# Third batch's keys taken into the second chunk's steps, and every second weight tile of layer 2 finished on GpSimd

## The chip, the cores and the metric

The kernel runs on one core of a Trainium2 chip. The core has TensorE (PE, matmuls and transposes into PSUM banks), VectorE (DVE), ScalarE (ACT), GpSimd (POOL) and SyncE (SP), which issues every DMA of this kernel from one queue. Each engine works through its own queue in order and waits on semaphores. The metric is the device time of one execution in microseconds.

## The reference

Eight batches of attention, whose keys and values are first averaged over groups of eight rows (576 rows become 72), feed two layers of the same shape: 4608 tokens, 512 wide, through 2048 and back.

```python
k_p = k.reshape(B, H, Sp, pool, D).mean(axis=3)      # v_p likewise
scores = scale * np.matmul(q, k_p.transpose(0, 1, 3, 2))
attn = softmax(scores);  x = np.matmul(attn, v_p)    # B*S = 4608 tokens, H*D = 512
h = np.maximum(x @ w_in, 0.0);   x = h * h @ w_out   # layer 1
h = x @ w_in2                                        # layer 2
g = np.where(h >= 1, h, np.where(h <= -1, 0.0, (h + 1) ** 2 / 4))
out = g @ w_out2
```

q, k and v are float32. The four weight matrices come as float64, so the kernel decodes them from their 64-bit words; each float32 factor of a large product is split into a rounded half and its residue, and three matmuls stand for one.

## The kernel before

**Tiling.** The 4608 tokens are nine chunks of 512 (`NC`). A batch has 576 tokens, so its border falls inside a chunk: the second chunk (tokens 512 to 1023) and the third (1024 to 1535) each span two batches. For each chunk and layer the 2048 inner columns are 16 steps (`KF`) of 128. A step is `h_mm` (L627: 12 matmuls, hp) and, two steps behind (`LAG`), `y1_mm` or `y2_mm` (L666, L677: 12 matmuls into the four result banks y0 to y3). Two hp banks alternate. Between the products stand the activation and the split: `act1` (L638: three ScalarE passes and one VectorE instruction, L652) in layer 1, `act2` (L655: three ScalarE passes, two VectorE instructions, L661 and L663) in layer 2. A result bank leaves through `y_out` (L686), alternately by ScalarE and VectorE, into one of two `yo` buffers and by a store; layer 1's result goes to DRAM (`x2T`) and comes back for layer 2 by `load_x2` and `split_x2` (L717).

**Weights.** Class `Weights` handles one layer. Tile f holds the 128 columns of w_in and the 128 rows of w_out of step f. `load` (L227) brings 1 MB by two DMAs into the slot of tile f; layer 2's tile f lies in layer 1's slot f - 1, so its load waits for the last product that reads layer 1's tile f - 1 (tile 0 has a buffer of its own, xb). `decode0` is two ScalarE passes (L256, L263), `decode1` four VectorE instructions (L269, L272, L275, L278), `split_hi` one ScalarE pass (L285), and `split_lo` (L288) one VectorE instruction, L290, the last of a tile: 1024 columns, both inputs and the output in SBUF. `stages` (L293) runs them as a pipeline: one `step` does split_hi of tile k - 1, decode0 of tile k + 1, decode1 of tile k, and split_lo of tile k - 1 inside that decode1. The first step does decode0 of tiles 0 and 1.

**Stages.** The opening (to about 177 us) does the first chunk's attention, layer 1's weights, the first chunk of layer 1, and the second chunk's attention, in an order that a list planner (`Order`, L49) chose from assumed durations and from the events that each chain waits for. Keys of a batch are loaded (`load_k`, L332, 288 KB for two heads) into one buffer `kv`, averaged by three GpSimd additions (`k_pool`, L365 to L369), then transposed and scaled (`k_T`, L379). `v_pool` and `v_split` do the like for values. In the planner's chain `keys1` (L869) the second batch's keys and values are followed by the third batch's four key pairs and its first value load. From the second chunk of layer 1 on, the attention of the next chunk is placed by hand: `attention_units` (L722) gives each unit a position in steps, and the main loop (L1034) emits those that are due (`do`) twice a step. In the last chunk of layer 1 the loop also calls `w2.load_to(f)` and, from step index 3 (`STEPS2`) on, `w2.step()`; in layer 2's first chunk the remaining steps follow, one per step (L1075).

Of the kernel before, what the change touches and what calls it, by code (L numbers as in the profile page):

```python
# [14 lines left out]
ALU = mybir.AluOpType  # L15
# [33 lines left out]
class Order:  # L49
# [13 lines left out]
    def add(self, gen, rank=0.0):  # L63
        c = [rank, self.now, gen, None, None]
        self.chains.append(c)
        self.go(c)
# [57 lines left out]
def pooled_attention_moe_moe2(  # L124
# [13 lines left out]
    nc = tc.nc  # L138
# [5 lines left out]
    NP = H // 2  # L144
# [30 lines left out]
    for d in range(2):  # L175
        m = mask[64 * d:64 * d + 64]
        nc.gpsimd.affine_select(
            out=m, in_=m, compare_op=ALU.is_ge, fill=0.0, base=0, channel_multiplier=1, pattern=[[-KL, H]]
        )
        nc.gpsimd.affine_select(  # L180
            out=m, in_=m, compare_op=ALU.is_ge, fill=0.0, base=KL - 1, channel_multiplier=-1, pattern=[[KL, H]]
# [7 lines left out]
    for c in range(NC):  # L189
        gs, col = [], 0  # L190
        while col < N:
            t0_ = c * N + col
            b, s = t0_ // S, t0_ % S
            n = min(S - s, N - col, NG)
# [12 lines left out]
    def w_tile(f, dtype, name):  # L207
        return wpool.tile([P, 4 * DM], dtype, tag=f"w{f}", name=name)

    class Weights:  # L210
# [76 lines left out]

        def split_lo(self, f, t):  # L288
            av = self.a.pop(f).rearrange("p (w n) -> p w n", w=2)
            nc.vector.tensor_tensor(out=t[:, :, 1], in0=av, in1=t[:, :, 0], op=ALU.subtract)  # L290
            self.ready.add(f)

        def stages(self):  # L293
# [35 lines left out]
    def kv_tile():  # L329
        return att.tile([P, 2, POOL * D], F32, tag="kv", name="kv")  # L330

    def load_k(b, p, t=None):  # L332

        t = kv_tile() if t is None else t
        nc.sync.dma_start(
            out=t[:SP_], in_=k[b, 2 * p:2 * p + 2].rearrange("h (s r) d -> s h (r d)", r=POOL)
        )
        kraw[b, p] = t

    def load_v(b, g, t=None):  # L340

        t = kv_tile() if t is None else t
        for e in range(2):
            r = slice(64 * e, 64 * e + 64)
            if g < 2:
                src = v[b, 4 * g + e:4 * g + e + 3:2, :KA * POOL, :]
                nc.sync.dma_start(out=t[r], in_=src.rearrange("h (s r) d -> s h (r d)", r=POOL))
            else:
                src = v[b, :, KA * POOL:, :]
                nc.sync.dma_start(out=t[r, 0], in_=src.rearrange("h (s r) d -> h s (r d)", r=POOL))  # L350
        vraw[b, g] = t
# [9 lines left out]
    def pool8(eng, t, dst):  # L361
        us = (("POOL", 1.3), ("POOL", 0.8), ("POOL", 0.7)) if eng is nc.gpsimd else (
            ("DVE", 0.7), ("DVE", 0.45), ("DVE", 0.3))
        yield us[0]
        eng.tensor_tensor(out=t[:, :, :256], in0=t[:, :, :256], in1=t[:, :, 256:], op=ALU.add)  # L365
        yield us[1]
        eng.tensor_tensor(out=t[:, :, :128], in0=t[:, :, :128], in1=t[:, :, 128:256], op=ALU.add)
        yield us[2]
        eng.tensor_tensor(out=dst, in0=t[:, :, :64], in1=t[:, :, 64:128], op=ALU.add)  # L369
# [3 lines left out]
    def k_pool(b, p, eng):  # L373
        kp = att.tile([P, 2, D], F32, tag="kp", name="kp", bufs=4)
        t, dst = kraw.pop((b, p))[:SP_], kp[:SP_]
        yield from pool8(eng, t, dst)
        kp_t[b, p] = kp
# [14 lines left out]
    def v_pool(b, g, eng):  # L392
        t = vraw.pop((b, g))
        w = 2 if g < 2 else 1
        vp = att.tile([P, 2, D], F32, tag="vp", name="vp") if b else lent[7][:, 0, 2 * D * g:2 * D * g + 2 * D]
        if b == 0:
            vp = vp.rearrange("p (a d) -> p a d", d=D)
        vp_t[b, g] = vp
        yield from pool8(eng, t[:, :w], vp[:, :w])
# [45 lines left out]
    w1, w2 = Weights(0), Weights(1)  # L445
# [3 lines left out]
    def at_once(chain):  # L449

        if chain is None:
            return
        value = None
        while True:
            try:
                kind, x = chain.send(value)
            except StopIteration:
                return
            value = None
            if kind == "take":  # L460
                value = order.things[x].pop(0)[1]
# [260 lines left out]
    def attention_units(c, at, stage=(0, 0.5, 1, 1, 2, 2.5, 3)):  # L722

        units = []
        ts = tiles[c]

        def add(s, f, *a):
            units.append((s, lambda: at_once(f(*a))))

        for i, T in enumerate(ts):  # L730
            s = at[i]
            if i:
                add(at[i - 1] + 0.5, load_q, T)
            else:
                add(s - 2, load_q, T)
            add(s + stage[0], t0, T)
            add(s + stage[1], t1, T, 0)
            add(s + stage[1], t1, T, 1)
            add(s + stage[2], t3, T)
            add(s + stage[3], t4, T)  # L740
            add(s + stage[4], t56, T)
            G = T.group
            if T is G.tiles[-1]:
                for p in range(NP):
                    add(s + stage[5 + p // 2], pv_pair, G, p)
            if i + 1 < len(ts) and ts[i + 1].b != T.b:

                b = T.b + 1
                a = s + stage[1]
                if b > 2:  # L750
                    add(a - 7, load_k, b, 0)
                for p in range(NP):
                    if b > 2:
                        add(a - 6 + 1.5 * p, k_pool, b, p, nc.gpsimd)
                        if p + 1 < NP:
                            add(a - 6 + 1.5 * p, load_k, b, p + 1)
                        else:
                            add(a - 6 + 1.5 * p, load_v, b, 0)
                    add(a + 0.5 + p // 2 * 0.5, k_T, b, p)
                e = s + stage[6]  # L760
                add(a, v_pool, b, 0, nc.gpsimd)
                add(a, load_v, b, 1)
                add(e, v_split, b, 0, nc.gpsimd)
                add(e, v_pool, b, 1, nc.gpsimd)
                add(e, load_v, b, 2)
                add(e + 1, v_split, b, 1, nc.gpsimd)
                add(e + 1, v_pool, b, 2, nc.gpsimd)
                add(e + 1.5, v_split, b, 2, nc.gpsimd)
        return units

    STEPS2 = 3

    SCALAR = range(2, 9)

    with tc.manual_schedule():

        lent = []
        for i in range(4):
            t = w_tile(KF - 4 + i, F32, "lent").rearrange("p (e a n) -> p e a n", e=2, a=2)
# [7 lines left out]
        t = w_tile(8, F32R, "lent")  # L787
# [7 lines left out]
        def comes(us):  # L795

            landed[0] = max(landed[0], order.now) + us
            return landed[0] + 2.0
# [70 lines left out]
        def keys1():  # L869
            for p in range(NP):  # L870
                load_k(1, p)
                yield "until", comes(1.3)
                yield from k_pool(1, p, nc.gpsimd)
                order.signal("kp", p)
            for g in range(3):
                load_v(1, g)
                yield "until", comes(2.2)
                yield from v_pool(1, g, nc.gpsimd)
                yield ev("x", G1[0])
                yield from v_split(1, g, nc.gpsimd)  # L880
            for p in range(NP):
                load_k(2, p)
                yield "until", comes(1.3)
                yield from k_pool(2, p, nc.gpsimd)
            load_v(2, 0)

        def keys1_T():
            yield ev("scores", T1[0])
# [134 lines left out]
        units = []  # L1023
        for c in range(2, NC):
            n = len(tiles[c])
            stride = 3 if n > 4 else 3.5
            units += attention_units(c, [16 * (c - 1) - 1 + stride * i for i in range(n)])
        units.sort(key=lambda u: u[0])

        def do(s):  # L1030
# [3 lines left out]
        for c in range(1, NC):  # L1034
            last = c + 1 == NC
            for f in range(KF):
                hp = h_mm(x_of(c), W[0, 0, f])
                outs(2)
                do(KF * c + f)
                if last and f == 0:  # L1040
                    att_cm.__exit__(None, None, None)
                    l2 = ctx.enter_context(tc.tile_pool(name="l2", bufs=1))
                if f >= LAG:
                    y_step(0, c, f - LAG)
                elif f == 0:
                    y_step(0, c - 1, KF - 1)
                at_once(act1(hp, c, f))
                outs(2)
                if last:
                    w2.load_to(f)  # L1050
                    if f == 3:
                        xraw = load_x2(0)
                    if f >= STEPS2:
                        w2.step()
                    if f in (8, 10, 12, 14):
                        split_x2(0, xraw, (8, 10, 12, 14).index(f))
                do(KF * c + f + 0.5)
            y_step(0, c, KF - 2)
            if last:
                w2.load_to(KF)  # L1060
# [58 lines left out]
```

## Time and profile before

| | |
|---|---|
| median of 3 runs | 1794.53 us (1792.99 to 1795.15) |
| the profiled execution's own time | 1792.96 us |
| its span | 1791.2 us |
| PE busy | 1743.7 us, 97% |
| DVE busy | 739.7 us, 41% |
| ACT busy | 781.4 us, 44% |
| POOL busy | 158.2 us, 9% |
| mean granted TensorE clock | 0.987 |

A row of the profile's views gives a start and a duration in us, counted from the span's start; "L290" is a line of the kernel, out<-in are tiles by name. A bracket behind a row is the time for which the engine stood idle before it, and what ended that. DVE's busy time is not even: in the 40 slices of the span (44.8 us each) it stands at 70%, 90% and 90% in the first three, at 20% to 40% in most, and at 90% and 80% in the two from 940 to 1030 us. Matmuls overlap, so a matmul's own duration (0.39) is longer than its place in the queue (0.23).

### The profile page before, as it was taken

What the parts mean: (1) busy time and instruction counts of PE and PEld (TensorE: products, weight loads), DVE (VectorE), ACT (ScalarE), POOL (GpSimd) and SP (SyncE); (2) the same over time, 40 slices, a digit from 0 to 9 for tenths busy, and PEclk for the clock granted to TensorE, in tenths of its full rate; (3) what the DMA queues carried; (4) which work ended last, traced back from release to release, by engine and by line L of the source; (5) the groups of instructions that cost most, each with busy time, mean ns of one, the idle gap of its engine ahead of it and who ended that gap; (6) DMA issues with size and microseconds to landing.
All of it is one profiled execution on the core that took longest, in us unless ns stands there. A gap on an engine that the chain in (4) does not pass through costs nothing.

```text
span 1791.2 us, 20650 instructions
## 1 busy us (share of the span) xinstructions
PE 1743.7 (97%) x8116; PEld 1442.2 (81%) x8116; DVE 739.7 (41%) x1234; ACT 781.4 (44%) x1499; POOL 158.2 (9%) x183
## 2 busy tenths in 40 slices
PE   5898999999999999999999999999999999999999
PEld 4676788888888888888888788888888888888887
DVE  7995433434243333433339832232332323233222
ACT  5874434434343343344348633333333333334333
POOL 3333211202021110300000000000000000000000
PEclk6999999999999999999999999999999999999999
DMA  9643201102021121201045301010101010101000
GB/s 252 182 123 100 55 23 53 41 26 65 13 70 28 50 48 34 52 18 36 1 142 196 133 1 47 1 47 1 47 1 47 1 47 1 48 1 48 0 24 24
DMA packets 89601, 95.18 MB, mean 53 GB/s; under 512 B 43296, under 2 KB 61984, under 8 KB 89504
## 3 DMA queue, kind: packets, MB, share of 16 engines
q1 hardware_dynamic: 89504, 93.87, 17.9%
q8 instruction: 64, 1.05, 0.2%
q14 instruction: 33, 0.27, 0.1%
HBM read 73.66 MB, written 20.19 MB: 52 GB/s over the span
## 4 chain that ended last, share of the span: by engine, by line
PE 87%; DVE 8%; DMA 2%; issue 2%; ACT 1%; SPq 0%; DVEq 0%; ACTq 0%
PE hp L633 14%; PE hp L634 13%; PE hp L635 13%; PE y L684 7%; PE y L682 7%; PE y L683 7%; PE y L671 7%; PE y L672 6%; PE y L675 6%; PE pvps L611 2%; PE sps L502 2%; DVE w L290 1%; DVE wa L275 1%; DVE wa L278 1%; DVE wa L269 1%
## 5 line engine op out<-in xcount | busy, mean ns | idle before, releaser
L633 PE MATMUL hp<-x,w 128*128 128x512 f32 x1116 | 442.5, 396 | 4.9 <-ACT w L285 2.7
L634 PE MATMUL hp<-x,w 128*128 128x512 f32 x1116 | 436.4, 391 | 0.6 <-DVE w L290 0.5
L635 PE MATMUL hp<-x,w 128*128 128x512 f32 x1116 | 436.6, 391 | 0.0
L633 PEld LDWEIGHTS hp<-x,w 128*128 128x128 f32 x1116 | 210.6, 189 | 49.5 <-ACT w L285 3.1
L661 DVE SCALAR_TENSOR_TENSOR u<-u,hp 128x512 f32<-128x512 f32 x144 | 99.0, 687 | 359.7 <-ACT u L660 359.7
L635 PEld LDWEIGHTS hp<-x,w 128*128 128x128 f32 x1116 | 210.4, 189 | 44.7
L634 PEld LDWEIGHTS hp<-x,w 128*128 128x128 f32 x1116 | 210.6, 189 | 42.8 <-DVE w L290 1.4
L671 PE MATMUL y<-gh,w 128*128 128x512 f32 x576 | 231.3, 402 | 0.0
L652 DVE TENSOR_TENSOR gl<-hp,gh 128x512 fp32r<-128x512 f32 x144 | 99.4, 690 | 310.7 <-ACT hp L650 310.5
L672 PE MATMUL y<-gh,w 128*128 128x512 f32 x576 | 225.1, 391 | 0.0
L659 ACT ACTIVATE u<-hp 128x512 f32<-128x512 f32 x144 | 85.9, 596 | 286.8 <-PE hp L635 286.8
L684 PE MATMUL y<-w,gl 128*128 128x512 f32 x540 | 210.2, 389 | 0.0
L682 PE MATMUL y<-w,gh 128*128 128x512 f32 x540 | 210.2, 389 | 0.0
L683 PE MATMUL y<-w,gh 128*128 128x512 f32 x540 | 210.1, 389 | 0.0
L662 ACT ACTIVATE gh<-u 128x512 fp32r<-128x512 f32 x144 | 91.0, 632 | 173.5 <-PE y L683 148.9
L663 DVE TENSOR_TENSOR gl<-u,gh 128x512 fp32r<-128x512 f32 x144 | 99.8, 693 | 157.8 <-ACT gh L662 152.2
L675 PE MATMUL y<-gl,w 128*128 128x512 f32 x576 | 154.4, 390 | 0.0
L648 ACT ACTIVATE gh<-hp 128x512 fp32r<-128x512 f32 x144 | 86.2, 598 | 120.3 <-PE y L672 119.4
L641 ACT ACTIVATE hp<-hp 128x512 f32<-128x512 f32 x144 | 85.0, 591 | 99.5 <-PE hp L635 99.2
L675 PEld LDWEIGHTS y<-gl,w 128*128 128x128 f32 x576 | 108.1, 188 | 23.0
L671 PEld LDWEIGHTS y<-gh,w 128*128 128x128 f32 x576 | 108.3, 188 | 21.0
L672 PEld LDWEIGHTS y<-gh,w 128*128 128x128 f32 x576 | 108.4, 188 | 20.3
(140 smaller groups left out, 2004.9 us busy)
## 6 DMA issues: line engine op xcount, KB each, us to landing
w<-in_moe_w_in_dram SPq DMA_DIRECT2D x31, 512.0 KB
w<-in_moe_w_out_dram SPq DMA_DIRECT2D x31, 512.0 KB
x2T<-yo SPq DMA_DIRECT2D x36, 256.0 KB
xraw<-x2T SPq DMA_DIRECT2D x9, 1024.0 KB
out_dram<-yo SPq DMA_DIRECT2D x35, 256.0 KB
qraw<-in_q_dram SPq DMA_DIRECT2D x32, 256.0 KB
kv<-in_k_dram SPq DMA_DIRECT2D x28, 288.0 KB
kv<-in_v_dram SPq DMA_DIRECT2D x28, 256.0 KB
```

The costliest lines, as they stand in the source:

```text
L633: nc.tensor.matmul(out=hp, lhsT=hi[:, cs], rhs=xh[kk], start=(kk == 0), stop=False)
L634: nc.tensor.matmul(out=hp, lhsT=lo[:, cs], rhs=xh[kk], start=False, stop=False)
L635: nc.tensor.matmul(out=hp, lhsT=hi[:, cs], rhs=xl[kk], start=False, stop=(kk == KD - 1))
L652: nc.vector.tensor_tensor(out=gl, in0=hp, in1=gh, op=ALU.subtract)
L661: nc.vector.scalar_tensor_tensor(out=u, in0=u, scalar=1.0, in1=hp, op0=ALU.min, op1=ALU.max)
L663: nc.vector.tensor_tensor(out=gl, in0=u, in1=gh, op=ALU.subtract)
L671: nc.tensor.matmul(out=ys[d], lhsT=hi[:, cs], rhs=gh, start=(f == 0), stop=False)
L672: nc.tensor.matmul(out=ys[d], lhsT=lo[:, cs], rhs=gh, start=False, stop=False)
L675: nc.tensor.matmul(out=ys[d], lhsT=hi[:, cs], rhs=gl, start=False, stop=(f == KF - 1))
L682: nc.tensor.matmul(out=ys[t], lhsT=gh[:, cs], rhs=hi, start=(f == 0), stop=False)
L683: nc.tensor.matmul(out=ys[t], lhsT=gh[:, cs], rhs=lo, start=False, stop=False)
L684: nc.tensor.matmul(out=ys[t], lhsT=gl[:, cs], rhs=hi, start=False, stop=(f == KF - 1))
```

## The change

`split_lo` of layer 2 goes to GpSimd for odd tiles. `STEPS2` falls from 3 to 2, so that the first `w2.step()` comes in the third step of layer 1's last chunk instead of the fourth, and tile 0 is loaded in the first step of it instead of the second. The third batch's key loads, key averages and first value load leave `keys1`; `attention_units` emits them for batch 2 too, starting with the second chunk's first step, 1.25 steps apart, and the third chunk's tokens from the second on are put about three steps later.

```diff
@@ -287,7 +287,9 @@
 
         def split_lo(self, f, t):
             av = self.a.pop(f).rearrange("p (w n) -> p w n", w=2)
-            nc.vector.tensor_tensor(out=t[:, :, 1], in0=av, in1=t[:, :, 0], op=ALU.subtract)
+
+            eng = nc.gpsimd if self.layer and f % 2 else nc.vector
+            eng.tensor_tensor(out=t[:, :, 1], in0=av, in1=t[:, :, 0], op=ALU.subtract)
             self.ready.add(f)
 
         def stages(self):
@@ -747,17 +749,22 @@
 
                 b = T.b + 1
                 a = s + stage[1]
-                if b > 2:
-                    add(a - 7, load_k, b, 0)
+                e = s + stage[6]
+                if b == 2:
+
+                    k0, gap, kt = s, 1.25, [s + 2.5 + 1.25 * p for p in range(NP)]
+                    a, e = s + 6, s + 7
+                else:
+                    k0, gap, kt = a - 7, 1.5, [a + 0.5 + p // 2 * 0.5 for p in range(NP)]
+                add(k0, load_k, b, 0)
                 for p in range(NP):
-                    if b > 2:
-                        add(a - 6 + 1.5 * p, k_pool, b, p, nc.gpsimd)
-                        if p + 1 < NP:
-                            add(a - 6 + 1.5 * p, load_k, b, p + 1)
-                        else:
-                            add(a - 6 + 1.5 * p, load_v, b, 0)
-                    add(a + 0.5 + p // 2 * 0.5, k_T, b, p)
-                e = s + stage[6]
+                    sp = (k0 + 0.5 if b == 2 else k0 + 1) + gap * p
+                    add(sp, k_pool, b, p, nc.gpsimd)
+                    if p + 1 < NP:
+                        add(sp, load_k, b, p + 1)
+                    else:
+                        add(sp, load_v, b, 0)
+                    add(kt[p], k_T, b, p)
                 add(a, v_pool, b, 0, nc.gpsimd)
                 add(a, load_v, b, 1)
                 add(e, v_split, b, 0, nc.gpsimd)
@@ -768,7 +775,7 @@
                 add(e + 1.5, v_split, b, 2, nc.gpsimd)
         return units
 
-    STEPS2 = 3
+    STEPS2 = 2
 
     SCALAR = range(2, 9)
 
@@ -878,11 +885,6 @@
                 yield from v_pool(1, g, nc.gpsimd)
                 yield ev("x", G1[0])
                 yield from v_split(1, g, nc.gpsimd)
-            for p in range(NP):
-                load_k(2, p)
-                yield "until", comes(1.3)
-                yield from k_pool(2, p, nc.gpsimd)
-            load_v(2, 0)
 
         def keys1_T():
             yield ev("scores", T1[0])
@@ -1024,7 +1026,10 @@
         for c in range(2, NC):
             n = len(tiles[c])
             stride = 3 if n > 4 else 3.5
-            units += attention_units(c, [16 * (c - 1) - 1 + stride * i for i in range(n)])
+            at = [16 * (c - 1) - 1 + stride * i for i in range(n)]
+            if c == 2:
+                at[1:] = [at[0] + 6.5 + 3 * i for i in range(n - 1)]
+            units += attention_units(c, at)
         units.sort(key=lambda u: u[0])
 
         def do(s):
@@ -1047,7 +1052,7 @@
                 at_once(act1(hp, c, f))
                 outs(2)
                 if last:
-                    w2.load_to(f)
+                    w2.load_to(f or 1)
                     if f == 3:
                         xraw = load_x2(0)
                     if f >= STEPS2:
```

## Rows read from the trace of the kernel before

**Rows 1.** Busy time by stretch: length, then PE, PEld, DVE, ACT, POOL busy, clock, DMA.

```profile
922.40:1003.99 81.59, 81.59 (x362) 67.56 (x360) 73.64 (x85) 67.33 (x89) 0.00 (x0) 1.00 0.61 209
1003.99:1030.10 26.11, 22.69 (x98) 17.79 (x97) 22.21 (x28) 16.38 (x23) 0.00 (x0) 1.00 0.24 81
```

**Rows 2.** Timeline of DVE in layer 1's last chunk: start, duration, instruction.

```profile
934.05 0.69 DVE L652 TENSOR_TENSOR gl<-hp,gh 128x512 fp32r<-128x512 f32 x1 [0.66 <-ACT hp L650]
...
940.12 0.69 DVE L269 TENSOR_SCALAR wa<-wa 128x1024 f32<-128x1024 f32 x1
...
941.45 1.22 DVE L290 TENSOR_TENSOR w<-wa,w 128x1024 fp32r<-128x1024 f32 x1
942.58 1.22 DVE L275 SCALAR_TENSOR_TENSOR wa<-w,wa 128x1024 int32<-128x1024 int32 x1
943.83 1.23 DVE L278 CUSTOM_DVE_ANT_0 wa<-w,wa 128x2048 uint16<-128x2048 uint16 x1
...
945.58 0.68 DVE L269 TENSOR_SCALAR wa<-wa 128x1024 f32<-128x1024 f32 x1
```

**Rows 3.** Groups by line, 929.3 to 1003.9: busy us, mean ns of one.

```profile
L256 ACT ACTIVATE wa<-w 128x1024 f32<-128x1024 f32 x13 | 14.9, 1143 | 0.0
...
L641 ACT ACTIVATE hp<-hp 128x512 f32<-128x512 f32 x12 | 7.0, 585 | 0.0
L720 DVE TENSOR_TENSOR x<-xraw,x 128x512 fp32r<-128x512 f32 x4 | 2.7, 685 | 0.0
```

**Rows 4.** Timeline of PE: a first product that needs the bank back.

```profile
938.71 0.39 PE L633 MATMUL hp<-x,w 128*128 128x512 f32 x1
```

**Rows 5.** Timeline of DVE in layer 2's first steps.

```profile
1004.56 0.68 DVE L269 TENSOR_SCALAR wa<-wa 128x1024 f32<-128x1024 f32 x1
...
1012.00 0.69 DVE L269 TENSOR_SCALAR wa<-wa 128x1024 f32<-128x1024 f32 x1
...
1018.92 0.69 DVE L269 TENSOR_SCALAR wa<-wa 128x1024 f32<-128x1024 f32 x1
```

**Rows 6.** Timeline of DVE in the opening, beside POOL.

```profile
32.57 2.24 DVE L278 CUSTOM_DVE_ANT_0 wa<-w,wa 128x2048 uint16<-128x2048 uint16 x1
...
144.63 1.75 DVE L275 SCALAR_TENSOR_TENSOR wa<-w,wa 128x1024 int32<-128x1024 int32 x1
```

**Rows 7.** Timeline of POOL: two rows beside DVE, two with DVE idle.

```profile
32.46 1.26 POOL L365 TENSOR_TENSOR kv<-kv 72x512 f32<-72x512 f32 x1 [6.42 <-DMA kv<-in_k_dram]
...
143.70 1.60 POOL L367 TENSOR_TENSOR kv<-kv 72x256 f32<-72x256 f32 x1
...
175.44 1.29 POOL L365 TENSOR_TENSOR kv<-kv 128x512 f32<-128x512 f32 x1 [20.32 <-DMA kv<-in_v_dram]
176.81 0.74 POOL L367 TENSOR_TENSOR kv<-kv 128x256 f32<-128x256 f32 x1
```

**Rows 8.** Timeline of SP's queue: tile 1 of layer 2.

```profile
922.58 0.38 SPq L232 DMA_DIRECT2D w<-in_moe_w_in_dram  x1
```

**Rows 9.** Busy time by stretch: last two numbers DMA share and GB/s.

```profile
927.00:928.00 1.00, 1.00 (x6) 0.84 (x5) 0.00 (x0) 0.82 (x2) 0.00 (x0) 1.00 0.17 70
```

**Rows 10.** Chain that ended last: start, length, piece.

```profile
124.92 5.32 DMA x1S<-xs
...
188.20 2.03 DMA x2T<-yo
```

**Rows 11.** Timeline of SP's queue in the opening.

```profile
124.14 0.50 SPq L335 DMA_DIRECT2D kv<-in_k_dram  x1
```

**Rows 12.** Timeline of ACT in the opening, with its wait.

```profile
130.35 0.39 ACT L619 ACTIVATE xs<-pvps 128x256 fp32r<-128x256 f32 x1 [3.26 <-DMA x1S<-xs]
```

**Rows 13.** Timeline of PE: waits in the opening and the second chunk's start.

```profile
139.94 0.63 PE L560 MATMUL aps<-ident,A 128*128 128x128 f32 x4 [1.87 <-DVE A L541]
...
182.86 0.26 PE L383 MATMUL kps<-ident,kp 72*128 72x72 f32 x1 [0.64 <-DVE E L521]
183.72 0.25 PE L383 MATMUL kps<-ident,kp 72*128 72x72 f32 x1 [0.60 <-DVE E L521]
```

## The prediction, made before the change was run

> **What bounds the kernel now.** I read four views, in this order: busy time by stretch, VectorE's instructions in order of time, GpSimd's beside them, and the chain of waits at the two places where TensorE stands still. TensorE works through 288 steps, each a first-product group and a second-product group of 12 matmuls. From 922.40 to 1003.99, in the last chunk of layer 1, 30 groups take 81.59 us: 2.72 each, 5.44 a step, with no gap [rows 1]. The next eight groups, over the seam into layer 2, take 26.11 where 8 x 2.72 = 21.76 would do, so 4.3 us are lost there [rows 1]; behind the seam the steps are whole again. The other loss lies in the opening. The two halves of the change touch one of them each.
>
> In the last chunk VectorE, not TensorE, is full. One step of it runs from the clamp at 940.12 to the next at 945.58, which is 5.46 us without a hole, and the instruction that the change moves (L290) holds the queue for 942.58 - 941.45 = 1.13 [rows 2]. Four of the steps carry one more instruction (L720), 0.60 each at its spacing [rows 3]. VectorE therefore loses 0.02 a step and 4 x 0.60 = 2.4 on TensorE. That is paid from slack: the residue (L652) that ends at 934.05 + 0.69 = 934.74 is first missed by the matmul at 938.71, 3.97 later [rows 2, 4]. In layer 2 the same decode meets a longer activation: VectorE's steps there go from 1004.56 to 1012.00 to 1018.92, 7.44 and 6.92 [rows 5], and this overrun is the 4.3 lost.
>
> **Layer 2's weights: GpSimd's instruction.** Eight of 16 tiles lose 1.13 us of VectorE's queue each, 9.0 in all. GpSimd's 128x512 addition takes 1.29 and its 128x256 one 0.74 when VectorE is idle [rows 7]; 0.55 per 256 columns more makes 1.29 + 2 x 0.55 = 2.39 for 1024 columns, which I take. What it does to VectorE is seen in the opening. While GpSimd's addition held 32.46 to 33.72, VectorE's L278, issued at 32.57, took 2.24 where it takes 1.23 alone; it ended at 34.81, about one clean duration after GpSimd's end [rows 6, 7]. L275 at 144.63 took 1.75 where its clean row has 1.22 [rows 2, 6]; GpSimd's L367 beside it, which had waited for VectorE in its turn, took 1.60 instead of 0.74 [rows 7]. So the two exclude one another, whole instructions at a time, for each of the decode's VectorE instructions that the rows show beside GpSimd. With VectorE always ready, an odd tile costs it 2.39 and saves 1.13: +1.26. The lower bound lets GpSimd run under the one residue per step that reads PSUM (0.60), a block of 1.79 and +0.66; below nothing it goes only if VectorE has holes, which is a rival.
>
> The GPSIMD Engine Reference of the Trainium skill (section "Performance versus the Vector engine") gives 4497 ns for such an addition over 2048 columns; half of it, 2.25, is an estimate from that page, and would make the layer-2 term below about 7.8 instead of 8.7.
>
> **Layer 2's weights: one step earlier.** Decoding from the third step gives VectorE one more step, but not a free one. Tile 1's slot is released when a second product ends, so its load leaves at 922.58 in either kernel [rows 8]; the transfer is at work until 927.2 or so [rows 9]. Today ScalarE comes to that tile a step later and finds it there. After the change ScalarE's in-order queue stands at it with the next step's three activation passes behind it, then that step's residue on VectorE. Two decode passes of 1.14 and three of about 0.59 [rows 3] put the third step's residue near 927.2 + 2.3 + 1.8 = 931.3. The fourth's stands behind that one (0.60) and a decode of 4.86 (5.46 less 0.60), near 936.7, which is 2.7 later than the row at 934.05 [rows 2]. Slack falls from 3.97 to 1.3. If the 1 MB input load that is issued just behind tile 2 delays it too, to about 0.1. Every later load is also waited for, with less than a step to spare. Tile 0's load, moved forward a step, goes between the stores of the chunk before, two issues of the size of the 0.38 in [rows 8], and I cost it at nothing. Nothing else is on GpSimd's queue by then. TensorE now waits on GpSimd for odd tiles, but first reads each one several steps after it is made, and ScalarE, which takes a tile's buffer over for the third tile after it, comes three steps later.
>
> **Sum for the seam.** Eleven steps remain in layer 1, 5.5 pairs. A pair has 2 x 5.46 + 1.26 = 12.18 on VectorE against 10.88 on TensorE: 5.5 x 1.30 = 7.2, and 2.4 for L720, less 1.3 of slack, is 8.3 of waiting already in layer 1, where today there is none. In layer 2 two decodes are left instead of three: (7.44 + 1.26 - 5.44) + (6.92 - 5.44) = 4.7. Together 13.0, less today's 4.3: **+8.7**. With a block of 1.79 the same sum gives 5.5 x 0.70 + 2.4 - 1.3 + 4.1 = 9.1, or **+4.8**. With late loads and the clean duration simply doubled (2.58), 8.2 + 2.4 - 0.1 + 4.9 = 15.4, or **+11**.
>
> **The keys: what leaves the opening.** Four key loads, a value load and twelve GpSimd additions leave. Two things there stand on the path to the last weight tile. A store of layer-1 input, issued at 124.92 right behind a key load of 124.14, needed 5.32 to land, where a store of the same size took 2.03 [rows 10, 11]; ScalarE stood 3.26 for it [rows 12], and TensorE later 1.87 for what follows [rows 13]. I take 1.87 of that as won, TensorE being otherwise busy. And VectorE's 0.53 at 144.63 goes [rows 6]. Together -2.4; at the least -0.5 (the store is slow by itself), at the most -3.8 (3.26 and 0.53). In the first step of the second chunk two key transposes sit on TensorE's queue and wait 0.64 and 0.60 for score banks [rows 13]. They now come steps later, one by one: -1.24, or 0 if another wait takes their place there.
>
> **The keys: what is added.** The same loads and additions in steps 16 to 22. GpSimd is idle there, and its additions at 1.29 + 0.74 and less collide with little on VectorE; I cost them at nothing. SyncE's queue is the cover to watch: each next key load waits for the addition that frees the one buffer, and the stores of layer 1's output are behind it, and behind these the four result banks of the next chunk. A landing of some 3 us and additions of 2.5 fit in the 5.44 between two such loads; at the bound, the landing of 5.32 [rows 10] with 2.5, each is 2.4 late, of which one would reach the banks: +2.4.
>
> **Total.** -2.4 - 1.24 + 8.7 = +5.1 on the profiled execution's own 1792.96 us (a span of 1791.2 and 1.8 around it), which is 1798.0. The median of the runs is 1794.53, 1.57 above that execution, so the forecast is 1799.6.
>
> **Rivals.** *GpSimd's instruction hides.* If VectorE has holes of its own while it waits for loads and for ScalarE, the block fills them and the whole 1.13 is won. The Perfetto Trace Analysis page of the Trainium skill ("Optimizing Scalar/DVE Operations") says that when VectorE is saturated, offloading, even to GpSimd, may help, and adds that between these two it might not; the rows here bear out the second. Against it: 5.46 of 5.44 us in use, and whole-instruction blocks. For it: eleven more steps with load waits. A microsecond less of block is worth 6.5 in the sum (5.5 pairs and the first step of layer 2), so the layer-2 part is zero at a block of 2.39 - 8.7/6.5 = 1.05, and the total at 2.39 - 5.1/6.5 = 1.6; below that the change is faster. Unblocked, most of the 4.3 goes: (7.44 - 1.13 - 5.44) is left in the first step, about -3.4, and with the keys' -3.6 the time is 1787.5. *The keys give nothing and the block binds.* The opening's store is as slow without the key load, or the moved loads hold SyncE's queue: 1794.53 + 8.7 - 0.5 = 1802.7, and with the moved loads' 2.4, 1805.1. *A near draw.* Block at its lower bound (+4.8), and the opening at its best (-3.8 - 1.24): 1794.5.
>
> **How the numbers follow.** The forecast's mechanism, with blocks of 1.79 to 2.58, has 0.58; its own range is 1794.5 (the draw's ends) to 1804 (+11 with -0.5 - 1.24). The hidden instruction has 0.20, keys that give nothing 0.12, the draw 0.10. About 0.2% (3.6 us) is what a measurement of this kernel can tell from no change. Slower by more: 0.40 of the 0.58 and the 0.12, so 0.52. Faster by more: 0.18 of the 0.20 and 0.06 of the draw, where more of the opening's waits close than I count: 0.24. Within: 0.24. The range reaches down to the hidden case and up past late keys: 1787.5 to 1806.
>
> **What would show it.** In the changed profile: VectorE's decode instructions of 3 us and more (1.2 plus a block) beside each GpSimd L290-like subtraction of about 2.4 in the last chunk; gaps on TensorE before first products from about two thirds of that chunk on; more than 4.3 lost at the seam; ScalarE waiting for a weight load in every step from the third on; in the opening no wait for a store near 127 to 130, and the last tile's load issued 2 to 3 us earlier. It would be wrong if VectorE's instructions keep their 1.2 beside GpSimd's, or if the steps of the last chunk stay at 5.44 to their end.

## The result, and the profile after

The changed kernel takes 1808.39 us (median of five runs, 1801.70 to 1809.11) beside 1795.15 for the kernel before (1792.99 to 1798.56): a ratio of 1.0058, interval 1.0044 to 1.0073, so 10.4 us slower. Run a second time beside other runs of before it gave 1.0052 (1.0035 to 1.0068), 9.3 us. The forecast was 5.1 us slower; the direction is right and half of the amount is missing. The median of 1808.39 lies 2.4 above the range's upper end; the ratio on the 1794.53 that was known then gives 1804.9, inside it.

The stretches that answer to [rows 1], in the same columns: 30 groups of the last chunk, eight groups over the seam, and the third and fourth of these eight.

```profile
927.05:1018.01 90.96, 83.66 (x361) 66.73 (x359) 84.71 (x82) 69.13 (x90) 14.46 (x6) 1.00 0.54 185
1018.01:1046.55 28.54, 25.36 (x96) 20.06 (x97) 18.54 (x21) 14.85 (x23) 5.08 (x2) 0.88 0.22 74
...
1027.99:1035.67 7.68, 7.68 (x25) 6.09 (x24) 6.56 (x8) 3.47 (x6) 0.00 (x0) 0.69 0.45 143
```

The 30 groups took 81.59 and now take 90.96; the eight took 26.11 and now take 28.54. That is 9.37 + 2.43 = 11.8. From there to the end the two profiles differ by 0.7 (761.13 and 760.47). VectorE in that chunk, which answers to [rows 2] (start, duration, instruction):

```profile
942.14 0.68 DVE L654 TENSOR_TENSOR gl<-hp,gh 128x512 fp32r<-128x512 f32 x1
...
943.46 2.90 DVE L272 TENSOR_SCALAR wa<-wa 128x1024 int32<-128x1024 int32 x1
946.40 1.22 DVE L275 SCALAR_TENSOR_TENSOR wa<-w,wa 128x1024 int32<-128x1024 int32 x1
...
950.12 0.69 DVE L272 TENSOR_SCALAR wa<-wa 128x1024 int32<-128x1024 int32 x1
950.73 1.22 DVE L292 TENSOR_TENSOR w<-wa,w 128x1024 fp32r<-128x1024 f32 x1
...
955.58 2.89 DVE L272 TENSOR_SCALAR wa<-wa 128x1024 int32<-128x1024 int32 x1
```

And GpSimd beside it, with what it waited for:

```profile
943.40 2.42 POOL L292 TENSOR_TENSOR w<-wa,w 128x1024 fp32r<-128x1024 f32 x1 [149.06 <-ACT w L285]
955.51 2.40 POOL L292 TENSOR_TENSOR w<-wa,w 128x1024 fp32r<-128x1024 f32 x1 [9.70 <-ACT w L285]
967.68 2.42 POOL L292 TENSOR_TENSOR w<-wa,w 128x1024 fp32r<-128x1024 f32 x1 [9.76 <-ACT w L285]
980.39 2.40 POOL L292 TENSOR_TENSOR w<-wa,w 128x1024 fp32r<-128x1024 f32 x1 [10.30 <-ACT w L285]
...
1035.68 2.40 POOL L292 TENSOR_TENSOR w<-wa,w 128x1024 fp32r<-128x1024 f32 x1 [12.87 <-PE y L685]
```

L272 takes 0.69 by itself and 2.90 beside GpSimd's subtraction: it ends at 946.36, which is 0.54 behind GpSimd's end (943.40 + 2.42 = 945.82), so nearly its whole clean duration comes after that. VectorE gives up 1.22 (L292) and pays 2.2 for it, in every second tile. The Trainium skill (SBUF — State Buffer, section "Who interferes with whom") says that the two engines share a port pair as an exclusive lock and that whoever issues first holds it for the whole instruction; these rows agree, with 2.90 for 0.69. ScalarE and TensorE, with their waits:

```profile
932.91 1.12 ACT L256 ACTIVATE wa<-w 128x1024 f32<-128x1024 f32 x1 [3.32 <-DMA w<-in_moe_w_out_dram]
938.00 1.16 ACT L256 ACTIVATE wa<-w 128x1024 f32<-128x1024 f32 x1 [0.39 <-DMA w<-in_moe_w_out_dram]
943.82 1.14 ACT L256 ACTIVATE wa<-w 128x1024 f32<-128x1024 f32 x1 [0.50 <-DMA w<-in_moe_w_out_dram]
```

```profile
949.54 0.50 PE L635 MATMUL hp<-x,w 128*128 128x512 f32 x1 [0.56 <-DVE gl L654]
...
1026.54 0.80 PE L684 MATMUL y<-xb,gh 128*128 128x512 f32 x1 [2.94 <-DVE yo L697]
...
1027.99 0.63 PE L635 MATMUL hp<-x,w 128*128 128x512 f32 x1
1028.42 0.63 PE L636 MATMUL hp<-x,w 128*128 128x512 f32 x1
```

TensorE now waits at first products from 949.54 on, where before it had waited for nothing in this chunk. At the seam it stands 2.94 for a result bank, and the matmuls behind that follow one another every 0.43, where 2.72 / 12 = 0.23 is usual: the lower clock of 1.2 GHz. The stretch 1027.99 to 1035.67 shows it as a granted clock of 0.69, with TensorE busy all the time; two groups (one step) that need 5.44 take 7.68.

### The profile page after: what moved, and what is told of

Its sections match the earlier page's. It is cut to its first block, busy times and chain, and to the rows that moved or that the text cites. A ratio compares the mean times of both kernels' runs of the same rounds, so it can differ in the third digit from the quotient of the medians.

```text
span 1807.0 us, 20671 instructions
## 1 busy us (share of the span) xinstructions
PE 1745.4 (97%) x8116; PEld 1442.5 (80%) x8116; DVE 740.9 (41%) x1226; ACT 781.1 (43%) x1499; POOL 173.6 (10%) x191
## 4 chain that ended last, share of the span: by engine, by line
PE 85%; DVE 8%; DMA 3%; ACT 2%; issue 2%; SPq 0%; DVEq 0%; ACTq 0%
PE hp L635 13%; PE hp L636 13%; PE hp L637 13%; PE y L684 7%; PE y L686 7%; PE y L685 7%; PE y L673 6%; PE y L674 6%; PE y L677 6%; PE pvps L613 2%; PE sps L504 2%; DVE wa L272 1%; DVE wa L275 1%; DVE w L292 1%; PE qps L486 1%
## 5 line engine op out<-in xcount | busy, mean ns | idle before, releaser
L654 DVE TENSOR_TENSOR gl<-hp,gh 128x512 fp32r<-128x512 f32 x144 | 99.4, 690 | 311.6 <-ACT hp L652 311.4
```

The source lines that it names most:

```text
L654: nc.vector.tensor_tensor(out=gl, in0=hp, in1=gh, op=ALU.subtract)
```

## The experiments

Two measures go together here. The ratio to the runs of before made beside each kernel holds everything, the chance variation of the opening too, and its interval is some 5 us wide. The lengths of the two stretches of [rows 1] hold the seam alone and repeat to some hundredths where VectorE isn't blocked. All seam figures below are the two lengths less 81.59 + 26.11 = 107.70. A ratio to before of 1.0010 is 1.8 us.

| kernel | 30 groups | 8 groups | seam | ratio to before |
|---|---|---|---|---|
| the change | 90.96 | 28.54 | +11.80 | 1.0058 (1.0044 to 1.0073) |
| the change again | 90.96 | 27.02 | +10.28 | 1.0052 (1.0035 to 1.0068) |
| layer 2's edits alone | 91.09 | 27.26 | +10.65 | 1.0046 (1.0031 to 1.0062) |
| GpSimd's instruction alone | 87.04 | 28.46 | +7.80 | 1.0039 (1.0022 to 1.0055) |
| earlier decode alone | 84.22 | 25.95 | +2.47 | 1.0003 (0.9985 to 1.0020) |
| GpSimd beside VectorE's own | 86.54 | 28.51 | +7.35 | 1.0034 (1.0022 to 1.0046) |
| keys alone, twice | 81.60 | 26.13 | 0.0 | 0.9987 (0.9972 to 1.0002); 1.0000 (0.9987 to 1.0013) |
| left-over decodes spread | 81.60 | 21.76 | -4.34 | 0.9976 (0.9962 to 0.9991) |
| keys and spread | 81.60 | 21.76 | -4.34 | 0.9966 (0.9953 to 0.9980) |
| keys, spread, one addition on VectorE | 81.60 | 21.76 | -4.34 | 0.9948 (0.9932 to 0.9963) |
| the same without the keys | 81.60 | 21.76 | -4.34 | 0.9969 (0.9956 to 0.9981) |

Part of five of these seam figures is TensorE's lower clock, whose length changes from run to run. Each matmul spaced 0.43 costs 0.20 more than one spaced 0.23; counted so, it is about 2.8 us in the change, 1.2 in its second profile, 1.4 each in layer 2's edits alone, GpSimd's instruction alone and GpSimd beside VectorE's own, and nothing in the others. Without it the seams are +9.0, +9.0, +9.3, +6.4 and +6.0, with +2.5 for the earlier decode.

**The parts by themselves.** Layer 2's two edits without the keys:

> Only layer 2's weights change: GpSimd does the subtraction of the odd tiles and the decode starts at the third step; the keys stay where they were. Forecast: 8.7 us slower than before. What the two traces suggest now: 11.8 slower (all of it between the 134th and the 150th group), 2 or so of it from TensorE's lower clock behind a wait of about 3 us at the seam. Rival (the 15.8 between the two profiles came mainly from the keys or from the whole program running otherwise): 0 to 5 slower. Second rival (the GpSimd instruction hides): faster by 3.

It measured 8.3 us slower (5.6 to 11.2), and its seam +10.65. So the change's loss is in these two edits, and neither the keys nor chance makes it. GpSimd's instruction, with the decode starting where it did:

```
-            nc.vector.tensor_tensor(out=t[:, :, 1], in0=av, in1=t[:, :, 0], op=ALU.subtract)
+            eng = nc.gpsimd if self.layer and f % 2 else nc.vector
+            eng.tensor_tensor(out=t[:, :, 1], in0=av, in1=t[:, :, 0], op=ALU.subtract)
```

> GpSimd does the subtraction of layer 2's odd tiles; the decode starts at the fourth step as before, and the keys stay. If the exclusive block is the price: each odd tile costs VectorE about 2.2 to 2.4 in its next instruction and saves 1.13, so +1.1 to +1.3 for each of some 6 odd tiles that are decoded before the queue runs free, and the step left for the end costs more: 7 to 9 us slower than before. If the earlier start is the price: within 2 us of before. If GpSimd's instruction hides: 3 us faster.

7.0 us slower (4.0 to 9.9), its seam +7.80: most of the loss is this line. And the earlier start alone:

```
-    STEPS2 = 3
+    STEPS2 = 2
...
-                    w2.load_to(f)
+                    w2.load_to(f or 1)
```

> Only the start of layer 2's decode moves from the fourth step of the last chunk to the third; VectorE does every subtraction and the keys stay. If the load of the second tile makes the early step worthless: slack falls by 2.7 to 3.9, and a step of 5.46 less is left behind the seam: 1 to 2.4 us slower than before. If the early step is a full step won: 4 us faster (the loss at the seam goes). If the earlier start were what costs the change its time: 8 or more slower.

0.5 us slower by the ratio, which can't be told from nothing; its seam loses 2.47, a little above the first bound. The early step costs instead of winning: VectorE has one step's work less behind the seam, but it begins the chunk without slack, and every later 0.02 and 0.60 of overrun now reaches TensorE. The row that shows it is ScalarE's, at the second tile:

```profile
929.13 1.12 ACT L256 ACTIVATE wa<-w 128x1024 f32<-128x1024 f32 x1 [3.34 <-DMA w<-in_moe_w_out_dram]
```

2.47 + 7.80 = 10.27, against 10.65, 10.28 and 11.80 for both; without the lower clock 2.5 + 6.4 = 8.9 against 9.0 to 9.3. The two parts add.

**Is it the block, or the hand-over to GpSimd?** VectorE keeps its whole subtraction, and GpSimd does half of it once more into a scratch that nobody reads:

```
             nc.vector.tensor_tensor(out=t[:, :, 1], in0=av, in1=t[:, :, 0], op=ALU.subtract)
+            if self.layer and f % 2:
+                s = l2.tile([P, DM], F32, tag="idle", name="idle")
+                nc.gpsimd.tensor_tensor(out=s, in0=av[:, 0], in1=t[:, 0, 0], op=ALU.subtract)
```

> Before, with one addition to the work: for every odd tile of layer 2 GpSimd also subtracts 512 of the 1024 columns into a scratch that nobody reads, while VectorE keeps its whole subtraction. So VectorE saves nothing and is only shut out, for one GpSimd instruction of 512 columns (1.29 on an idle VectorE) for each odd tile. If the exclusive block is the price: 1.1 to 1.3 more for each pair of steps, a pair of 12.1 against 10.88 on TensorE, so 7 to 9 us slower than before, like the run in which GpSimd takes the whole of the odd tiles' subtraction. If the hand-over to GpSimd (TensorE's and ScalarE's waits for its result) were the price: no difference, since nobody waits for the scratch.

6.1 us slower (3.9 to 8.3), its seam +7.35. Nobody waits for the scratch, so the block alone costs this much (+6.0 without the lower clock). GpSimd and VectorE in this kernel:

```profile
942.41 1.30 POOL L293 TENSOR_TENSOR idle<-wa,w 128x512 f32<-128x512 f32 x1 [151.17 <-ACT w L285]
954.49 1.84 POOL L293 TENSOR_TENSOR idle<-wa,w 128x512 f32<-128x512 f32 x1 [10.78 <-ACT w L285]
966.50 1.73 POOL L293 TENSOR_TENSOR idle<-wa,w 128x512 f32<-128x512 f32 x1 [10.18 <-ACT w L285]
```

```profile
942.42 1.84 DVE L272 TENSOR_SCALAR wa<-wa 128x1024 int32<-128x1024 int32 x1
...
954.48 0.69 DVE L272 TENSOR_SCALAR wa<-wa 128x1024 int32<-128x1024 int32 x1
955.09 2.32 DVE L290 TENSOR_TENSOR w<-wa,w 128x1024 fp32r<-128x1024 f32 x1
```

The first pair of steps takes 954.49 - 942.41 = 12.08, as the change's takes 955.51 - 943.40 = 12.11. At 954.49 it is GpSimd that loses first (1.84 for 1.30), and then VectorE (2.32 for 1.22). VectorE's part is 1.10 there and 1.15 at 942.42 (1.84 for 0.69), and the second pair takes 966.50 - 954.49 = 12.01: the price is about the same whoever is first.

**The keys alone.** The diff's parts in the key units and in the opening, without layer 2's:

> Only the third batch's keys move; VectorE keeps every subtraction of layer 2's decode and the decode starts at the fourth step, as before. Forecast's theory: 2.4 won in the opening and 1.24 at the second chunk's first step, some 3.6 us faster than before, nothing given back later. What the two traces suggest now: 3.4 won up to the 16th first product, some 2.7 more in steps 16 and 17 and 1.9 to 2.6 given back in step 18, so 3.5 faster as well, with the half of it in other places. Rival (the moved loads hold SyncE's queue, or the opening's store is slow by itself): between 0.5 faster and 2 slower. The seam stays at 26.1 us for its eight groups. The fifth first product starts at about 80 or about 88 us by chance, since the kernels do the same until then.

2.3 us faster, with an interval over zero, so it was run once more:

> The keys alone once more, since 2.3 us faster [5.0 faster to 0.4 slower] left open whether they give anything. Forecast's theory: 3.6 faster. From the profiles so far (kernels with moved keys stand 2.4 to 4.0 better at the 40th first product than at the fifth, but those without stand up to 2.5 better there too, when their fifth began late): about 1 to 2 faster. Rival: no difference. In the profile the third key tile's last addition on GpSimd takes either under 1 us, and the fifth first product begins by 83, or nearly 5, and it begins near 87.

No difference (2.3 either way). The traces tell where the gain goes. Starts of first products in TensorE's timeline, as means over profiles of kernels with the keys moved (five: the change twice, keys alone twice, keys and spread) and with the keys where they were (seven, before twice among them):

| | to the 10th | 10th to 16th | 16th to 33rd |
|---|---|---|---|
| keys in the opening | 115.8 | 48.1 | 123.3 |
| keys moved | 119.8 | 44.9 | 124.3 |

Between the 10th and the 16th first product the moved keys win 3.2, and the second chunk takes 1.0 of it. The rows show one longer wait there, first with the keys moved (keys alone, first profile), then before:

```profile
189.27 0.33 PE L611 MATMUL pvps<-AH,VH 128*128 128x128 f32 x1 [2.95 <-DVE AL L572]
```

```profile
191.69 0.33 PE L611 MATMUL pvps<-AH,VH 128*128 128x128 f32 x1 [1.43 <-DVE AL L572]
```

The two transposes' waits of [rows 13] are gone, but their 1.24 isn't won: this wait is 1.5 longer. It is 2.90 to 2.95 in the six profiles with moved keys and 1.30 to 1.47 in the eight without. What else goes into the 1.0 wasn't traced. Then there is the first column, 4.0 later, though up to there the engines do the same work in the same order in all these kernels, but for one key load on SyncE's queue. It is three late profiles that make it: without them, the moved keys stand at 116.7 there, 0.9 later.

**The late opening.** In the first profile of the change the fifth first product began at 87.87, in that of before at 79.71.

> The changed kernel a second time. In its first profile the fifth first product began at 87.87 us, where it begins between 79.7 and 83.0 in the five other profiles, though all these kernels do the same work in the same order until then. If this is chance, it begins this time between 79.7 and 83 with the odds of the five, the seam again loses 11.8 more than before, the keys give some 3.5 back, and the run stands 8 above before. If the change causes it, by where its code or its transfers lie, it begins near 88 again, and the run stands 12 to 16 above before.

> Before, a second profile. If the lock-out of GpSimd's addition and the late fifth first product come by chance in every kernel, this profile shows one of two pictures: the addition under 1 us and the fifth first product by 83, with a time of 1790 to 1796, or nearly 5 and near 86, with 1797 to 1801. If it needs the moved keys, the first. The seam loses 4.3 in both.

The change was late again (86.28), before was not (79.72), so its profile bears out the second picture; but its runs stand 9.3 above before, not 12 to 16. Among all fourteen profiles three are late (86.28 to 87.87) and eleven are not (78.32 to 83.00), and the three share one row. GpSimd in the change's second profile, where the last addition of this third key tile (72x128) takes 0.46 to 0.93 in the profiles that aren't late:

```profile
57.63 1.29 POOL L367 TENSOR_TENSOR kv<-kv 72x512 f32<-72x512 f32 x1 [3.88 <-DMA kv<-in_k_dram]
58.99 0.74 POOL L369 TENSOR_TENSOR kv<-kv 72x256 f32<-72x256 f32 x1
59.81 4.79 POOL L371 TENSOR_TENSOR kp<-kv 72x128 f32<-72x128 f32 x1
```

The same stretch in the second profile of before:

```profile
54.36 1.51 POOL L365 TENSOR_TENSOR kv<-kv 72x512 f32<-72x512 f32 x1 [3.37 <-DMA kv<-in_k_dram]
55.95 1.06 POOL L367 TENSOR_TENSOR kv<-kv 72x256 f32<-72x256 f32 x1
57.09 0.92 POOL L369 TENSOR_TENSOR kp<-kv 72x128 f32<-72x128 f32 x1
```

And VectorE beside the late one:

```profile
60.21 0.27 DVE L548 TENSOR_TENSOR lent<-lent,sm 64x128 f32<-64x128 f32 x1
60.41 1.21 DVE L275 SCALAR_TENSOR_TENSOR wa<-w,wa 128x1024 int32<-128x1024 int32 x1
61.55 1.21 DVE L292 TENSOR_TENSOR w<-wa,w 128x1024 fp32r<-128x1024 f32 x1
62.68 1.21 DVE L278 CUSTOM_DVE_ANT_0 wa<-w,wa 128x2048 uint16<-128x2048 uint16 x1
63.82 0.67 DVE L654 TENSOR_TENSOR gl<-hp,gh 128x512 fp32r<-128x512 f32 x1
64.42 0.73 DVE L269 TENSOR_SCALAR wa<-wa 128x1024 f32<-128x1024 f32 x1
```

Here GpSimd is the one shut out, by VectorE's instructions following each other without a hole. The next key load waits for this addition, the loads queued on SyncE wait behind it, and a store of layer-1 input comes to stand among them; ScalarE pays, in the change's second profile and in before's first:

```profile
85.55 0.22 ACT L621 ACTIVATE xs<-pvps 128x64 fp32r<-128x64 f32 x1 [10.17 <-DMA x1S<-xs]
```

```profile
79.03 0.22 ACT L619 ACTIVATE xs<-pvps 128x64 fp32r<-128x64 f32 x1 [2.76 <-DMA x1S<-xs]
```

What decides is who comes first: before's addition was through at 57.09 + 0.92 = 58.01, and here it came at 59.81, just ahead of VectorE's run. All three late profiles are of kernels with moved keys: three of the five with this opening, and none of the seven with the keys where they were. Before's own runs spread over 9 to 13 us in every large set, so late openings need not be theirs alone; whether the moved keys make them more frequent stays open. A test that takes the lock-out away, on top of two gains that come next:

**A version without the loss.** Before, with only this edit in layer 2's first chunk:

```
-                if c == 0:
+                if c == 0 and f % 3 == 2:
                     w2.step()
```

> Before, with the decodes that are left over at the seam done in every third step of layer 2's first chunk (third, sixth, ninth and twelfth), not one in each of its first steps; nothing on GpSimd, nothing earlier, keys as before. If VectorE's overrun in layer 2's first steps (7.44 and 6.92 against 5.44) is the whole 4.3 lost at the seam: one decode in three steps fits, and the kernel is 4 us faster, with eight groups from 1004 to 1030 in about 22. If the seam's loss comes from something else (the result banks, the input's load): no difference.

4.3 us faster (1.6 to 6.8), and the eight groups take 21.76, the full 4.34 less:

```profile
921.06:1002.66 81.60, 81.60 (x362) 67.59 (x360) 73.58 (x84) 67.16 (x88) 0.00 (x0) 1.00 0.62 210
1002.66:1024.42 21.76, 21.76 (x98) 18.02 (x96) 12.32 (x17) 11.89 (x19) 0.00 (x0) 1.00 0.29 98
```

So the whole loss at the seam came from the decodes that are left being due one in each step, and it needed no other engine: they were merely due too early. The test spreads their ScalarE passes along with VectorE's. That VectorE is the one that overruns is read from its rows, where it is busy but for 0.70 to 0.76 a step, in which it waits for ScalarE between its two activation instructions. With the keys moved as well:

> The keys moved as in the change, and the left-over decodes spread over every third step of layer 2's first chunk; no GpSimd instruction and no earlier start. If the two places are independent, the gains add: 2.3 to 3.9 from the keys and 4 from the seam, 6 to 8 us faster than before. If the measured keys' gain was chance: 4 faster.

6.1 us faster (3.6 to 8.4), at the lower end of what was expected. With the starved addition moved to VectorE in addition:

```
-        yield us[2]
-        eng.tensor_tensor(out=dst, in0=t[:, :, :64], in1=t[:, :, 64:128], op=ALU.add)
+        yield ("DVE", 0.3) if swap else us[2]
+        (nc.vector if swap else eng).tensor_tensor(out=dst, in0=t[:, :, :64], in1=t[:, :, 64:128], op=ALU.add)
...
-        yield from pool8(eng, t, dst)
+        yield from pool8(eng, t, dst, swap=b == 1 and p == 2)
```

> The combined kernel (keys moved, left-over decodes spread), with one more edit in the opening: the last of the three additions of the second batch's third key tile (72x128) goes from GpSimd to VectorE. In the three profiles whose fifth first product began near 87 us, this addition took 4.79 on GpSimd, with VectorE's instructions running without a hole beside it, where it takes 0.46 to 0.92 in the seven others. If that lock-out is what makes late runs late, they go: the combined kernel's times fall into two groups, 1785 to 1789 and 1791 to 1793, and here all lie in one, with a spread of some 4 us, and the fifth first product begins before 83. If the late runs come from the loads (each addition waits for its key tile), the two groups stay. The order of the work just behind the edit changes with it, so the level itself may move by a few us either way.

9.3 us faster than before (6.6 to 12.2): 1784.94, the fastest kernel here. The fifth first product begins at 78.32. But six runs spread from 1781.59 to 1788.94, not over the 4 us expected, and the opening's order changed with the edit, so the lock-out's share in the 3.2 us more isn't settled. The same without the moved keys:

> The best kernel so far (left-over decodes spread, the third key tile's last addition on VectorE) without the moved keys: batch 3's keys are pooled in the opening again, as before. The best kernel with moved keys stands at a ratio of 0.9948 to before. If the keys give their 3.6 us: 0.9968 here. If the keys give nothing, and the gain beyond the seam's 4.3 came from the re-ordered opening: 0.9948 here as well, within 0.0015. In the profile the seam's eight groups take 21.8 in either case; the 17th first product, which stands at 169.4 with moved keys, tells how much of the opening's gain is there without them: 169 to 170 by the rival, 172 to 173 by the forecast's theory.

5.6 us faster (3.4 to 7.9), at the number of the forecast's theory: with this opening the keys are worth 0.9969 - 0.9948, or 3.8 us, though the two intervals leave 0.2 to 7.4. Here twelve runs spread over 4.4 us (1788.27 to 1792.70), where those of the spread kernel took 11.0. The 17th first product stood at 179.42, where neither theory had put it: the single profile's opening was a later one.

That profile says more on the lock-out. GpSimd comes to the third key tile as late as in the late profiles, and the tile's last addition is now VectorE's:

```profile
59.79 0.72 POOL L367 TENSOR_TENSOR kv<-kv 72x256 f32<-72x256 f32 x1
65.03 1.57 POOL L365 TENSOR_TENSOR kv<-kv 72x512 f32<-72x512 f32 x1 [4.52 <-DMA kv<-in_k_dram]
```

```profile
60.54 0.29 DVE L369 TENSOR_TENSOR kp<-kv 72x128 f32<-72x128 f32 x1 [3.28 <-POOL kv L367]
```

The addition before the last stands at 58.99 to 60.21 in the three late profiles, and the next key tile's first one at 68.86 to 70.02; here it comes at 65.03, and the fifth first product at 82.12, not at 86 or later. So in this profile the edit did what it was meant to, at the price of a 3.28 wait on VectorE. It is a single profile, and in one without a lock-out (keys alone, first) that addition stood at 58.93, so whether it would have been late otherwise isn't shown.

## Why the prediction was half right

**What binds, right.** Behind the seam the decodes' overrun was the 4.3 lost, as the spread kernel shows; that it had no room in the last chunk, the kernels with a block show.

**GpSimd's instruction, right.** It takes 2.40 to 2.42 in seven of eight tiles (2.68 in the one where VectorE was first), estimated 2.39. A pair of steps on VectorE takes 955.58 - 943.46 = 12.12 against the 12.18 of the sum. The opening's rows that the forecast read showed the custom instruction and L275 blocked; here it is L272, at 2.78 to 2.96 a little under the 3 us named as the sign. The first rival, an instruction that hides, needed a block under 1.6 for any gain, and the block is 2.2.

The estimate of 2.25 that the prediction drew from the Trainium skill (GPSIMD Engine Reference, "Performance versus the Vector engine") lies 0.16 below the row.

**The earlier start, right in kind, too mild in size.** The slack was to fall from 3.97 to 1.3. The residue at 942.14 ends at 942.82; the matmul that misses it stands at 938.71 [rows 4] plus the 4.66 by which the opening was late, 943.37. So 0.55 is left. The load that ScalarE waits for landed later than I took from [rows 9]: ScalarE starts on it at 932.91, and an issue as in [rows 8] stands at 922.58 + 4.66 = 927.24, which makes 5.67 of it, not some 4.6. The 30 groups lose 9.37 and not 8.3; of the 1.1 more the smaller slack gives 0.75, and the rest wasn't traced. I had also expected the gaps from two thirds of the chunk on, against my own sum: they begin right behind GpSimd's first subtraction, at 949.54. And ScalarE waits for loads at three tiles, not at every one.

**The seam in layer 2: a term was missing.** Forecast 4.7. The eight groups lose 28.54 - 21.76 = 6.78. Less the 7.68 - 5.44 = 2.24 of lower clock in the second step that is 4.54, close to the forecast, but that is luck: all of it lies in the first step, where 3.26 was forecast, and some 0.6 of it is lower clock too (three matmuls from 1026.54 to 1027.99). That leaves 3.9 for the first step, and the 1.48 forecast for the second doesn't show. The clock is what the sum left out: a wait of 2.94 for a result bank, then a stretch at half speed, 2.8 in all, and 1.2 in the change's second profile. Even whether such a wait is followed by the lower clock varies. At the same matmul, GpSimd's instruction alone and the earlier decode alone both wait 1.81; the next matmuls are spaced 0.43 in the one and 0.23 in the other:

```profile
1017.01 0.79 PE L683 MATMUL y<-xb,gh 128*128 128x512 f32 x1 [1.81 <-DVE yo L696]
```

```profile
1014.93 0.51 PE L682 MATMUL y<-xb,gh 128*128 128x512 f32 x1 [1.81 <-DVE yo L695]
```

Together: 8.7 + 1.1 in the last chunk + 2.8 of clock - 0.8 (3.9 for 4.7) comes to 11.8, the figure of the first profile.

**The keys, the step that failed.** The opening's -2.4 came, as -3.2, and the last weight tile's load leaves 31.1 to 31.9 us behind the tenth first product with this opening and the keys moved, 33.7 to 34.3 with the keys where they were: 2 to 3 earlier, as named. The rest did not: the waits of 1.24 in the second chunk were replaced by another wait, which the forecast had kept as its other end ("or 0") and not taken; the chunk gave 1.0 away. Net 2.2 by the traces where 3.6 was forecast, not counting the late openings; by measurements 2.3 and 0.0 alone, 1.8 on top of the spread decodes (0.9976 to 0.9966) and 3.8 with the re-ordered opening. Only the last of these is clear of zero. TensorE's 1.87 falls to 0.92 or less in each of the six profiles with moved keys (1.45 to 1.89 in the seven with the same opening without). But the store wait of [rows 12] stays (1.92 and 2.57 in the two profiles of keys alone), so the key load in front of that store was not its whole cause. Nor does TensorE's wait follow the store's: before's second profile has 2.26 and 1.69, keys alone's second 2.57 and 0.92. So the 1.87 was won in large part, but not by the way through the store that the forecast gave; what won it stays open.

**The sum.** Against the 5.1 forecast, 9.3 and 10.4 were measured. The last chunk gives 1.1 of the difference, the clock 1.2 to 2.8, the keys 1.4, and the two steps of layer 2 take 0.8 off; about 1 remains, and a late opening more often than in before's runs would be enough for it, which isn't shown. Of the rivals, the one in which the keys give nothing and the block binds (1802.7 to 1805.1) came nearer than the forecast did, at a chance of 0.12: its half on the block was the forecast's own. (The draw's own sum, 4.8 - 3.8 - 1.24 on 1794.53, is 1794.3 and not 1794.5, which changes nothing.)

## What to carry to other kernels

Before you give an instruction from a full VectorE to GpSimd, set what GpSimd's instruction will block there against what VectorE gives up: here 2.2 stood against 1.2 in every second tile, and it cost 7.8 us, some 1.4 of it by the lower clock. Where a queue overruns its step, look first at when its work is due: the same work, spread over steps that have room, won the whole 4.3 us. And where TensorE will stand, count the slower matmuls that may follow as well as the stand.

## What the runs showed of the hardware

The lock holds both ways, and can hold for longer than one instruction. A GpSimd addition that takes 0.46 by itself took 4.79 in three profiles, while VectorE ran L548, L275, L292 and L278 without a hole. Its end at 59.81 + 4.79 = 64.60, less 0.46, is 64.14, inside L654, which reads one of its two operands from PSUM: it seems to have got in there. The Trainium skill (SBUF — State Buffer, "Who interferes with whom") says that a VectorE instruction with at most one SBUF input, outside the modes that use both of its ports, doesn't contend, which agrees with that time. The fourteen traces agree as well: this residue (L652 before, gl<-hp,gh) runs beside a GpSimd instruction on two tensors 404 times, 325 of them for at least half its length, and never takes more than its usual 0.69, where L272, with a single SBUF input, goes up to 2.96. That it was the residue that let GpSimd in was worked out and not tried.

A VectorE that is idle, but for one such instruction that keeps its 0.69, doesn't make GpSimd's 1024-column subtraction faster: 2.40 at 1035.68, as beside a blocked VectorE.

```profile
1036.78 0.69 DVE L663 SCALAR_TENSOR_TENSOR u<-u,hp 128x512 f32<-128x512 f32 x1 [1.41 <-ACT u L662]
```
